# Batch 4's second product as seven products of half blocks

## The chip, the cores and the metric

The kernel runs on one core of a Trainium2 chip. The metric is the device time of one execution in microseconds (us), lower is better; it is compared as the median of several runs. TensorE (PE, with its weight loads PEld), VectorE (DVE), ScalarE (ACT), GpSimd (POOL) and SyncE (SP, which issues all transfers here) run side by side; each takes its own instructions in the order of the program and waits on semaphores for the others.

## What is computed

Attention with a narrow window and block summaries gives x for 4 batches of 768 tokens by 512 channels; then a mix over tokens and two products with weights follow, in float32:

```python
x = attention(q, k, v)                       # (4, 768, 512)
u = x + (x.transpose(0, 2, 1) @ U @ V).transpose(0, 2, 1)
ch = np.maximum(u @ w_ch1, 0.0) @ w_ch2      # 512 -> 2048 -> 512
return (u + ch).astype(np.float32)
```

## The kernel before

**Precision.** Every operand of the two products is split into a high and a low part (a rounded copy by ACT, the rest by a subtraction on DVE or POOL). A product is three matmuls: high by high, high by low, low by high. The channels lie in 4 tiles of 128 (NC), the hidden layer in 16 (NF), a batch's tokens in two halves of 384 (NH).

**Batch 1** (b = 0) does each half of the tokens apart: for f in 0..15 and both halves, `up` (L983, 12 matmuls of 384 columns), `up_out` (ACT's gh at L995, DVE's gl at L996), `down_rows` (L1005, 9 matmuls of 512 columns). Beside it the weights are read as 64-bit words, turned into float32 (L155 on POOL, L161 and L164 on DVE), split (L179 on ACT, L180 on POOL) and stored back to HBM. DVE also makes sums of blocks of the first weight matrix (`sum_weights`, L901 to L905, two additions of 256 columns in each half of an even f). So the later batches load ready sums and only split them.

**Batches 2 to 4** (b = 1 to 3) each have two stages. `up_phase` is the first product by seven products of half blocks (a Strassen-Winograd form): for each of 8 pairs p of hidden tiles, seven products of 6 matmuls of 384 columns (L1271), whose sums ACT and DVE build in a tile (L1293 to L1331). `down_phase` is the second product in the ordinary form: for each f the hidden tile is gated (ACT's gh at L1340, DVE's gl at L1344), and 24 matmuls add to eight banks of PSUM (L1372), 12 of 512 columns and 12 of 256; `leave` (L1395) adds u and sends the output. Weights come through `fetch_weight` (a load into one of three places), `prepare` (the split of half a load, ACT at L179 and POOL at L180, into one of eight places) and `use_weight`; `tick` issues the next load some steps after a load was used up.

**What sets the order.** Everything is emitted by hand, step by step: a generator of the phase yields after each group of matmuls, and between two yields the loop puts the next batch's steps (`later_step`: attention, transposed rows, `mix`; `operands`: the seven operands of the next first product, with L754, L808, L796), spread evenly by `spread`. The last two half-block products of a first product (`last`) run inside the second. In batch 4 no next batch is left, so DVE, ACT and POOL have only the product's own work. Tiles that share a tag share memory; an instruction that writes one waits for the last reader of the tile before it.

## Time and profile before

| what | value |
|---|---|
| median of 3 runs (643.06 to 646.5) | 643.48 us |
| span of the profiled execution, first to last instruction | 644.2 us |
| mean granted TensorE clock, share of full speed | 0.996 |
| PE busy, share of the span | 623.3 us, 97% |
| DVE, ACT, POOL busy | 376.6, 348.2, 362.4 us |
| matmuls | 5480 |

Busy times are unions: a matmul of 384 columns lasts 337 ns from issue to its last result, but the next one starts long before that. So what a matmul costs is read from how many end in a stretch, not from its duration. The same is true of DVE where one instruction follows another without a wait.

### The profile page before, as it was taken

To read this page: it belongs to the slowest core of one execution; us is meant where nothing else is said; L and a number is where in the kernel's file an instruction comes from. 1 tells how busy PE (TensorE), PEld (TensorE's weight loads), DVE (VectorE), ACT (ScalarE), POOL (GpSimd) and SP (SyncE) were. 2 spreads that over 40 slices of the span, in tenths; PEclk is the share of its full clock that TensorE was granted. 3 is DMA by queue.
4 is the path that set the end of the run, shared out by engine and by line. 5 is a ranking of instruction groups with operands and counts; after the bars stand their busy time and mean duration, and the time that the engine had idled before them with its cause. 6 is when DMAs were issued, how large, how long until landed. Compare 5 with 4: busy or idle time off the path is not lost.

```text
span 644.2 us, 14528 instructions
## 1 busy us (share of the span) xinstructions
PE 623.3 (97%) x5480; PEld 560.6 (87%) x5480; DVE 376.6 (58%) x1026; ACT 348.2 (54%) x772; POOL 362.4 (56%) x391
## 2 busy tenths in 40 slices
PE   4979999999999999999999999999999999999997
PEld 3769988889888899998888899998888899998886
DVE  4869777675767596576555845567555722242223
ACT  3756666656564656665543467765453455553220
POOL 3524977965676776772247675772345565653320
PEclk9989999999999999999999999999999999999999
DMA  9897588766676269887786377887743164342102
GB/s 237 212 385 209 166 287 277 226 195 202 196 230 193 67 196 289 245 268 212 235 220 181 105 223 219 263 238 228 237 150 118 59 204 136 115 131 65 34 1 98
DMA packets 74437, 121.67 MB, mean 189 GB/s; under 512 B 7552, under 2 KB 48384, under 8 KB 74368
## 3 DMA queue, kind: packets, MB, share of 16 engines
q1 hardware_dynamic: 74368, 120.75, 61.8%
q8 instruction: 43, 0.70, 0.4%
q14 instruction: 26, 0.21, 0.1%
HBM read 93.45 MB, written 27.26 MB: 187 GB/s over the span
## 4 chain that ended last, share of the span: by engine, by line
PE 87%; DMA 4%; DVE 4%; SPq 2%; ACT 1%; issue 1%; POOL 0%; ACTq 0%; DVEq 0%
PE acc L1372 30%; PE ps_h L1271 27%; PE acc L1005 10%; PE ps_h L983 9%; PE ps_x L517 3%; PE ps_s L374 2%; PE ps_s L351 2%; DMA place<-in_w 2%; PE ps_t L487 1%; DMA kt<-in_k 1%; SPq L215 1%; DMA place<-in_q 1%; DMA place<-in_v 1%; PE ps_m L701 1%; DVE tmp L808 1%
## 5 line engine op out<-in xcount | busy, mean ns | idle before, releaser
L180 POOL TENSOR_TENSOR parts<-whole,parts 128x512 fp32r<-128x512 f32 (+1 forms) x144 | 182.6, 1276 | 153.2 <-ACT parts L179 143.6
L1372 PE MATMUL acc<-gh,parts 128*128 128x256 f32 (+1 forms) x768 | 198.1, 340 | 0.0
L1271 PE MATMUL ps_h<-op,parts 128*128 128x384 f32 x1008 | 181.7, 337 | 0.1
L1271 PEld LDWEIGHTS ps_h<-op,parts 128*128 128x128 f32 x1008 | 174.3, 188 | 2.7 <-issue 1.1
L1372 PEld LDWEIGHTS acc<-gh,parts 128*128 128x128 f32 x768 | 132.8, 189 | 17.9 <-issue 1.7
L1372 PE MATMUL acc<-gl,parts 128*128 128x256 f32 (+1 forms) x384 | 129.9, 338 | 2.5 <-DVE gl L1344 2.5
L1344 DVE SCALAR_TENSOR_TENSOR gl<-place,gh 128x768 fp32r<-128x768 f32 x48 | 52.8, 1101 | 60.7 <-ACT gh L1340 60.4
L179 ACT CAST parts<-whole 128x512 fp32r<-128x512 f32 (+1 forms) x144 | 83.3, 583 | 2.4 <-issue 1.1
L1372 PEld LDWEIGHTS acc<-gl,parts 128*128 128x128 f32 x384 | 72.8, 190 | 9.9 <-DVE gl L1344 3.2
L1340 ACT ACTIVATE gh<-place 128x768 fp32r<-128x768 f32 x48 | 40.5, 845 | 63.8 <-PE acc L1372 60.8
L410 ACT ACTIVATE e<-e,neg 128x120 f32<-128x120 f32 x144 | 46.5, 386 | 52.5 <-DVE neg L400 52.4
L983 PE MATMUL ps_h<-place 128*128 128x384 f32 x384 | 74.2, 341 | 0.0
L983 PEld LDWEIGHTS ps_h<-place 128*128 128x128 f32 x384 | 66.3, 188 | 1.2 <-issue 0.4
L1005 PE MATMUL acc<-place,gh 128*128 128x512 f32 x192 | 67.2, 405 | 0.0
L155 POOL TENSOR_SCALAR val<-place 128x512 f32<-128x512 f32 (+1 forms) x30 | 47.6, 1604 | 25.6 <-ACT place L142 21.4
L180 POOL TENSOR_TENSOR place<-val,place 128x512 fp32r<-128x512 f32 x29 | 38.7, 1353 | 18.3 <-ACT place L179 18.3
L796 POOL TENSOR_TENSOR op<-tmp,op 128x384 fp32r<-128x384 f32 x24 | 25.9, 1088 | 40.3 <-ACT op L792 39.2
L1005 PEld LDWEIGHTS acc<-place,gh 128*128 128x128 f32 x192 | 35.9, 188 | 7.5 <-POOL place L180 0.5
L400 DVE CUSTOM_DVE_ANT_0 e<-ps_s,mask_sb 128x120 f32<-128x120 f32 x144 | 32.7, 276 | 11.4 <-PE ps_s L351 5.9
L1005 PE MATMUL acc<-place,gl 128*128 128x512 f32 x96 | 37.8, 393 | 0.1
L1297 DVE TENSOR_TENSOR place<-place,ps_h 128x384 f32<-128x384 f32 x24 | 13.2, 550 | 36.8 <-PE ps_h L1271 36.8
L1331 DVE TENSOR_TENSOR place<-place,ps_h 128x384 f32<-128x384 f32 x24 | 13.3, 554 | 35.3 <-ACT place L1330 35.2
(122 smaller groups left out, 812.7 us busy)
## 6 DMA issues: line engine op xcount, KB each, us to landing
place<-in_w SPq DMA_DIRECT2D x32, 512.0 KB, 5.3
whole<-up SPq DMA_DIRECT2D x24, 512.0 KB, 4.2
whole<-down SPq DMA_DIRECT2D x24, 512.0 KB, 4.3
whole<-up SPq DMA_DIRECT2D x24, 384.0 KB, 3.5
vt<-in_v SPq DMA_DIRECT2D x48, 146.2 KB, 3.9
kt<-in_k SPq DMA_DIRECT2D x24, 288.0 KB, 5.3
there<-squares SPq DMA_DIRECT2D x16, 384.0 KB, 4.4
at<-there SPq DMA_DIRECT2D x64, 96.0 KB, 3.9
```

Source lines behind the costliest of these rows:

```text
L155: nc.gpsimd.tensor_scalar(f32(bits), f32(hi), 0.0, None, ALU.mult)
L179: nc.scalar.copy(hi, val)
L180: engine.tensor_tensor(lo, val, f32(hi), ALU.subtract)
L400: nc.vector.tensor_tensor_reduce(out=e[:, u, :], in0=ps[:, i * KC : (i + 1) * KC], in1=mask_sb[:, m, :], scale=-SCALE, scalar=BIG, op0=ALU ...
L410: nc.scalar.activation(e[:, u, :], e[:, u, :], AF.Exp, bias=st.neg[h][:, u : u + 1], scale=-1.0,)
L796: engine.tensor_tensor(by_tiles(t[:, 1]), by_tiles(val), by_tiles(f32(t[:, 0])), ALU.subtract)
L983: nc.tensor.matmul(ps[:, :NH], w_split[0, f][:, c % 2, part_w, c // 2], ut[:, c, :], start=(n == 0), stop=(n == 3 * NC - 1),)
L1005: nc.tensor.matmul(acc[t], gt[:, sl], w_split[1, f][:, part_w], start=(first and j == 0), stop=(last and j == 2),)
L1271: nc.tensor.matmul(ps, a[:, sa, i], b[:, sb, i], start=(first and n == 0), stop=(n == 5), skip_group_check=not first,)
L1340: nc.scalar.activation(gh, h, AF.Relu)
L1344: nc.vector.scalar_tensor_tensor(gl, h, 0.0, f32(gh), ALU.max, ALU.subtract)
L1372: nc.tensor.matmul(place, w[:, part_w, c * P : (c + 1) * P], gt[:, q0:q1], start=(f == 0 and i == 0 and j == 0), stop=(f == NF - 1 and j = ...
```

## The change

In batch 4 alone (`SEVEN = (3,)`) the second product is also made by seven products of half blocks. The second weight matrix is cut into blocks of two hidden tiles by 256 output channels. The products, in order, are A11 with B11, A12 with B21, S1 with T1, S2 with T2, S4 with B22, S3 with T3, A22 with T4; A and S are blocks and sums of weights, B and T blocks of the gated hidden layer and their sums. Each has 8 steps of 6 matmuls of 384 columns (4 groups of two hidden tiles, two tiles of 128 output channels).

- **Weights.** In batch 1 DVE makes the sums S1 to S4 (`sum_down`, four additions of 256 columns in each odd f, two in either half) and SP stores them (`store_down_sums`). In batch 3 the split parts of A11, A12 and A22 are stored from their places as they stand (`tick`, 24 transfers), so batch 4 loads them ready. The split of the sums in batch 4 has its low parts on DVE.
- **Operands.** 56 operands (7 names by 8 pairs p) are made by `second_operand`: for T1 to T4 first a sum in place on DVE, then a high part on ACT, then the low part on DVE, which is put behind the next operand's sum. 19 operands are made in the first product (`EARLY`), 6 of the sums for T1 too (`TURNED`). The rest go one or two a step, as far ahead as `lead` and the ring of 33 places allow. ReLU is applied where ACT copies a block out of PSUM, with one more pass for one of the four.
- **Outputs.** After each product DVE adds its two banks to u in x (L1621), or for the last addition of an output into a tile that is sent (L1624): 16 additions in place of the 8 of `leave`, one for each step.
- **Order and places.** Operand and hidden places are cut into two tiles each; transposed rows use operand places in place of hidden ones; for batch 4 the rows, their fetches and the first operands come some steps later in batch 3 (`ROWS`, `FETCH`, `JOIN`).

```diff
+_X = (("A11", "B11", "x"), ("A12", "B21", "y"), ("S1", "T1", "z"), ("S2", "T2", "x"), ("S4", "B22", "z"))
+_Y = (("S3", "T3", "x"), ("A22", "T4", "y"))
+SECOND = {2: (_X[0], _X[2], _X[1], _X[3], _X[4], _Y[1], _Y[0]), 3: _X + _Y}
+ADDED = {
+    "B11": ((0, 0),), "B21": ((0, 0),), "T1": ((1, 1),), "T2": ((0, 1),), "B22": ((0, 1),),
+    "T3": ((1, 1), (1, 0)), "T4": ((1, 0),),
+}
+PARTS = {"A11": (0, 0), "A12": (1, 0), "A22": (1, 1)}
...
+SUMS = ("S1", "S2", "S4", "S3")
+SEVEN = (3,)
...
+PARTS_IN = {1: (), 2: tuple(range(NF // 2))}
+AHEAD_UNITS = (45, 50)
+EARLY = {7 * p + 3 : p for p in range(8)} | {7 * p + 8 : 8 + p for p in range(7)}
+EARLY |= {7 * p + 13 : 16 + p for p in range(4)}
+FIRST_OPERANDS = [EARLY[i] for i in sorted(EARLY)]
+TURNED = {7 * p + 12 : p for p in range(6)}
...
+    ROWS = {2: {16: 0, 18: 1, 25: 2, 29: 3}, 3: {21: 0, 23: 1, 25: 2, 29: 3}}
+    FETCH = {2: {19: 0, 21: 1, 28: 2, 31: 3}, 3: {24: 0, 26: 1, 28: 2, 31: 3}}
+    JOIN = {2: (25, 27, 29, 31), 3: (28, 30, 32, 35)}
...
+        for i, t in enumerate(w_sums[p]):
+            nc.sync.dma_start(out=up_there[p][:, (4 + 4 * i) * P : (8 + 4 * i) * P], in_=t)
...
+        if b in SEVEN:
+            for name, _, _ in SECOND[b]:
+                if name in SUMS:
+                    units += [(("second", name, g), len(loads) + g // 2) for g in range(4)]
+                    loads += [down_sums[:, SUMS.index(name), 4 * j : 4 * j + 4] for j in range(2)]
+                else:
+                    units += [(("second", name, g), None) for g in range(4)]
+            tag_of += [unit_tags[n % 8] for n in range(28)]
...
+        if load is None:
+            _, name, g = key
+            t = wt.tile([P, 2 * DM], F32R, name="parts", tag=tag_of[n])
+            t = t.rearrange("p (m s c) -> p m s c", s=2, c=HC)
+            nc.sync.dma_start(out=f32(t), in_=down_parts[name][:, 2 * g : 2 * g + 2])
+            prepared.append((key, t))
+            return
...
+        split(hi, lo, whole, nc.vector if key[0] == "second" else nc.gpsimd)
         prepared.append((key, t))
+        pass_of = 1 if n < 3 * NF else 2
+        if key[0] == "down" and key[1] // 2 in PARTS_IN[pass_of]:
+            storing.append([3, key[1], t])
         if second:
...
+        for x in storing:
+            x[0] -= 1
+        if storing and storing[0][0] <= 0:
+            _, f, t = storing.pop(0)
+            for name, (odd, half) in PARTS.items():
+                if odd == f % 2:
+                    nc.sync.dma_start(
+                        out=down_parts[name][:, f // 2], in_=f32(t[:, :, half * HC : (half + 1) * HC])
+                    )
         due[:] = [n - 1 for n in due]
...
+    def sum_down(p, n):
+        (a11, a21), (a12, a22) = (
+            (x[:, :HC], x[:, HC:]) for x in (w_kept["down", f] for f in (2 * p, 2 * p + 1))
+        )
+        t = sts[0].x[:, 2 * (p % 3) + n]
+        down_out[p, n] = t
+        x, y = t[:, :HC], t[:, HC:]
+        if n == 0:
+            nc.vector.tensor_tensor(x, a21, a22, ALU.add)
+            nc.vector.tensor_tensor(y, x, a11, ALU.subtract)
+        else:
+            nc.vector.tensor_tensor(x, a12, down_out[p, 0][:, HC:], ALU.subtract)
+            nc.vector.tensor_tensor(y, a11, a21, ALU.subtract)
+    down_out = {}
...
+    def store_down_sums(p):
+        for n in range(2):
+            nc.sync.dma_start(
+                out=down_sums[:, 2 * n : 2 * n + 2, p],
+                in_=down_out[p, n].rearrange("p (m c) -> p m c", c=HC),
+            )
...
+            if st.b in SEVEN:
+                nc.scalar.activation(c[1][:, 0], x, AF.Relu)
+            else:
+                nc.scalar.copy(c[1][:, 0], x)
...
+            nc.scalar.copy(c[0][:, 1], x)
+            if st.b in SEVEN:
+                nc.scalar.activation(c[0][:, 0], c[0][:, 0], AF.Relu)
...
+    def first_sum(st, p):
+        a, b = st.h[p][0][:, 0], st.h[p][0][:, 1]
+        nc.vector.scalar_tensor_tensor(b, b, 0.0, a, ALU.max, ALU.subtract)
...
+    def second_operand(st, m):
+        n, p = divmod(m, NF // 2)
+        block, name, _ = SECOND[st.b][n]
+        c = st.h[p]
+        a, b, c, d = c[0][:, 0], c[0][:, 1], c[1][:, 0], c[1][:, 1]
+        st.gates[m] = hi, lo = st.ring[m]()
+        nv = nc.vector
+        if name == "T1" and p not in st.turned_first:
+            first_sum(st, p)
+        elif name == "T2":
+            nv.scalar_tensor_tensor(b, d, 0.0, b, ALU.max, ALU.subtract)
+        elif name == "T3":
+            nv.tensor_tensor(a, b, a, ALU.subtract)
+        elif name == "T4":
+            nv.tensor_tensor(c, c, b, ALU.subtract)
+        val = {"B11": a, "B21": c, "B22": d, "T1": b, "T2": b, "T3": a, "T4": c}[name]
+        def high():
+            if name == "B22":
+                nc.scalar.activation(hi, val, AF.Relu)
+            else:
+                nc.scalar.copy(hi, val)
+        def low():
+            if name == "B22":
+                nv.scalar_tensor_tensor(lo, val, 0.0, f32(hi), ALU.max, ALU.subtract)
+            else:
+                (nc.gpsimd if m in POOL_LOWS else nv).tensor_tensor(lo, val, f32(hi), ALU.subtract)
+        st.lows.append(low)
+        if len(st.lows) > 1:
+            st.lows.pop(0)()
+        high()
+    def second_start(st):
...
+        for m in FIRST_OPERANDS + [m for m in range(8 * len(OPS)) if m not in FIRST_OPERANDS]:
+            last = 2 * (m // 2) + 1
+            k = min(range(len(places)), key=lambda k: (free_at[k], k))
+            st.ring[m] = places[k][0]
+            st.ready[m] = free_at[k] + 1
+            free_at[k] = last
+        st.order = list(st.ring)
...
+    def second_phase(st):
+        while st.lows:
+            st.lows.pop()()
+        banks = {}
+        for i in range(8 * len(OPS)):
+            g, c = divmod(i, 2)
+            n, q = divmod(g, 4)
+            block, name, to = SECOND[st.b][n]
+            fresh = name not in ("T2", "B22", "T3")
+            if c == 0:
+                w = use_weight("second", block, q)
+            if fresh and q == 0:
+                banks[to, c] = half_bank(f"acc{to}{c}")
+            ps = banks[to, c]
+            for j in range(2):
+                gate = st.gates[2 * g + j]
+                for k, (sa, sb) in enumerate(((0, 0), (0, 1), (1, 0))):
+                    nc.tensor.matmul(
+                        ps,
+                        w[j][:, sa, c * P : (c + 1) * P],
+                        gate[sb],
+                        start=fresh and q == 0 and j == 0 and k == 0,
+                        stop=q == 3 and j == 1 and k == 2,
+                        skip_group_check=not fresh,
+                    )
+            yield
+            for more in range(2):
+                lead = (20 if i % 2 == 0 else -1, 6)[more]
+                while st.order and st.ready[st.order[0]] <= i and st.order[0] <= i + lead:
+                    second_operand(st, st.order.pop(0))
+                    if not more:
+                        break
+            if not st.order:
+                while st.lows:
+                    st.lows.pop()()
+            if late and i > late[0][0]:
+                finish_late()
+            if q == 3:
+                second_out(st, i + 1, n, c, ps)
+            if c == 0:
+                prepare()
+    late = []
+    def finish_late():
+        _, f, *args = late.pop(0)
+        f(*args)
...
+    def second_out(st, i, n, c, ps):
+        def add(mu, nu, ps, last):
+            ch = 2 * mu + c
+            kept = channel_rows(st, ch)[:, 3 * nu : 3 * nu + 3]
+            val = ps.rearrange("p (u q) -> p u q", q=P)
+            if not last:
+                nc.vector.tensor_tensor(kept, kept, val, ALU.add)
+                return
+            o = mo.tile([P, DM], F32, name="o", tag="val", bufs=VALS)[:, :NH]
+            nc.vector.tensor_tensor(o.rearrange("p (u q) -> p u q", q=P), kept, val, ALU.add)
+            late.insert(0, (i, send, ch, nu, o))
+        def send(ch, nu, o):
+            t0 = st.b * S + nu * NH
+            nc.sync.dma_start(out=out[ch, :, t0 : t0 + NH], in_=o)
+        order = [name for _, name, _ in SECOND[st.b]]
+        for to in ADDED[order[n]]:
+            last = not any(to in ADDED[name] for name in order[n + 1 :])
+            late.append((i, add, *to, ps, last))
     def leave(st, acc, q0, q1, channels):
...
+            if b in SEVEN:
+                if i == 0:
+                    second_start(cur)
+                if i in TURNED:
+                    first_sum(cur, TURNED[i])
+                if i in EARLY:
+                    second_operand(cur, cur.order.pop(0))
+                if i in AHEAD_UNITS:
+                    prepare()
+                continue
             if i == UP - 8:
```

In batch 1, around the operands of batch 2 in f = 13, this is what stands on DVE (L161 to L164 make weights, L996 is gl, `tmp` and `op` are operands). Before:

```order
L164 SCALAR_TENSOR_TENSOR val_2215<-place_2068,val_2215 128x512
L996 SCALAR_TENSOR_TENSOR gl_2382<-ps_h_2368,gh_2381 128x384
L808 TENSOR_TENSOR tmp_2409<-x_1456,ps_u_2402 128x384
L808 TENSOR_TENSOR tmp_2410<-tmp_2311,ps_u_2402 128x384
L796 TENSOR_TENSOR op_2235<-ps_u_2402,op_2235 128x384
L161 SCALAR_TENSOR_TENSOR val_2364<-place_2133,val_2364 128x512
L996 SCALAR_TENSOR_TENSOR gl_2442<-ps_h_2428,gh_2441 128x384
L161 SCALAR_TENSOR_TENSOR val_2365<-place_2182,val_2365 128x512
L808 TENSOR_TENSOR tmp_2311<-ps_u_2465,tmp_2410 128x384
```

And in the changed kernel, at the same place:

```order
L180 SCALAR_TENSOR_TENSOR val_2265<-place_2113,val_2265 128x512
L1084 SCALAR_TENSOR_TENSOR gl_2430<-ps_h_2416,gh_2429 128x384
L1050 TENSOR_TENSOR x_120<-val_2148,val_2265 128x256
L1051 TENSOR_TENSOR x_120<-x_120,val_2148 128x256
L824 TENSOR_TENSOR tmp_2460<-x_1482,ps_u_2452 128x384
L824 TENSOR_TENSOR tmp_2461<-tmp_2358,ps_u_2452 128x384
L812 TENSOR_TENSOR place_2457<-ps_u_2452,place_2457 128x384
L177 SCALAR_TENSOR_TENSOR val_2412<-place_2178,val_2412 128x512
L1084 SCALAR_TENSOR_TENSOR gl_2497<-ps_h_2483,gh_2496 128x384
L177 SCALAR_TENSOR_TENSOR val_2413<-place_2230,val_2413 128x512
L1053 TENSOR_TENSOR x_120<-val_2265,x_120 128x256
L1054 TENSOR_TENSOR x_120<-val_2148 128x256
```

Two additions stand behind one gl and two behind the next part of the weights; nothing else moved there.

In batch 4's second product DVE had one gl for each f and, at the end, the output's additions. Before:

```order
L1344 SCALAR_TENSOR_TENSOR gl_7834<-place_7282,gh_7833 128x768
L1344 SCALAR_TENSOR_TENSOR gl_7865<-place_7351,gh_7864 128x768
L1344 SCALAR_TENSOR_TENSOR gl_7896<-place_7351,gh_7895 128x768
L1395 TENSOR_TENSOR o<-acc_7496,x 128x512
L1395 TENSOR_TENSOR o<-acc_7500,x 128x512
```

In the changed kernel, while operands for the fourth product (S2 with T2) are made: L1504 is the sum for T2, L1520 an operand's low part, L196 a weight's low part, L1624 an output's addition.

```order
L1504 SCALAR_TENSOR_TENSOR place_7156<-place_7157,place_7156 128x384
L1520 TENSOR_TENSOR gate_7846<-place_7098,gate_7846 128x384
L196 TENSOR_TENSOR parts_7871<-whole_7665,parts_7871 128x2x256
L1504 SCALAR_TENSOR_TENSOR place_7235<-place_7236,place_7235 128x384
L1520 TENSOR_TENSOR gate_7867<-place_7156,gate_7867 128x384
L1624 TENSOR_TENSOR o_7891<-x_5610,accy0_7796 128x384
L196 TENSOR_TENSOR parts_7893<-whole_7825,parts_7893 128x2x256
L1504 SCALAR_TENSOR_TENSOR place_7316<-place_7317,place_7316 128x384
L1520 TENSOR_TENSOR gate_7887<-place_7235,gate_7887 128x384
```

Each operand's low part now stands behind the sum of the next operand, with a weight's low part and an output's addition between.

On SP in batch 3's second product, transfers for batch 4 (`kt`, `qz`, `there`, `at`, `vt`) and weight loads (`whole`) stood one after another. Before:

```order
L940 DMA whole_5948<-down3_109 128x1024
L435 DMA there_5957<-squares_5918 128x768
L443 DMA at_5959<-there_5769 32x4x192 x4
L229 DMA vt_5987<-in_v 96x390
L230 DMA vt_5987<-in_v 96x390
L940 DMA whole_6006<-down4_110 128x1024
```

In the changed kernel:

```order
L979 DMA whole_6277<-down_113 128x1024
L1027 DMA halfA11_114<-parts_6301 128x2x256
L449 DMA there_6385<-squares_6355 128x768
L457 DMA at_6387<-there_6230 32x4x192 x4
L245 DMA vt_6415<-in_v 96x390
L246 DMA vt_6415<-in_v 96x390
L1027 DMA halfA12_115<-parts_6379 128x2x256
L1027 DMA halfA22_116<-parts_6379 128x2x256
L979 DMA whole_6440<-down_113 128x1024
```

Three stores for each pair of hidden tiles (halfA11, halfA12, halfA22) now stand between them.

## Rows read from the trace of the kernel before

**Rows 1.** Page: busy us (share of the span) xinstructions of the engines.

```profile
PE 623.3 (97%) x5480; PEld 560.6 (87%) x5480; DVE 376.6 (58%) x1026; ACT 348.2 (54%) x772; POOL 362.4 (56%) x391
```

**Rows 2.** Stretches: length, then PE, PEld, DVE, ACT, POOL busy (xinstructions), PEclk, DMA share, GB/s.

```profile
60.00:217.00 157.00, 155.85 (x1236) 138.08 (x1235) 110.94 (x276) 95.39 (x225) 114.85 (x105) 1.00 0.67 209
...
515.28:571.28 56.00, 56.00 (x325) 56.00 (x324) 15.56 (x28) 30.37 (x62) 35.09 (x31) 1.00 0.48 150
571.28:640.42 69.14, 69.14 (x397) 61.05 (x396) 19.65 (x24) 20.19 (x30) 20.45 (x14) 1.00 0.16 54
640.42:644.16 3.74, 0.00 (x0) 0.00 (x0) 0.46 (x2) 0.00 (x0) 0.00 (x0) 0.82 0.43 140
```

**Rows 3.** Waits of PE, whole span: line <- releaser: us in total, times, longest.

```profile
PE acc L1372 <- DVE gl L1344: 2.5, 2, 1.3
```

**Rows 4.** Chain that ended last, in order of time: start us, us, what.

```profile
515.28 56.16 PE ps_h L1271 x324
...
576.31 64.12 PE acc L1372 x372
```

**Rows 5.** DVE in order of time, batch 3's second product: start us, us, instruction.

```profile
479.05 0.56 DVE L754 TENSOR_TENSOR x<-ps_u,place 128x384 f32<-128x384 f32 x1 [0.58 <-PE ps_u L751]
479.65 0.56 DVE L808 TENSOR_TENSOR tmp<-x 128x384 f32<-128x384 f32 x1
480.12 0.55 DVE L808 TENSOR_TENSOR tmp<-tmp,x 128x384 f32<-128x384 f32 x1
480.59 0.55 DVE L796 TENSOR_TENSOR op<-x,op 128x384 fp32r<-128x384 f32 x1
...
505.84 1.56 DVE L808 TENSOR_TENSOR tmp<-x 128x384 f32<-128x384 f32 x1
```

**Rows 6.** DVE by line and form, 511 to 645 us: busy us, mean ns | idle before.

```profile
L1395 DVE TENSOR_TENSOR o<-acc,x 128x512 f32<-128x512 f32 x8 | 5.1, 682 | 1.6 <-PE acc L1372 1.6
L1331 DVE TENSOR_TENSOR place<-place,ps_h 128x384 f32<-128x384 f32 x8 | 4.4, 555 | 17.3 <-ACT place L1330 17.3
```

**Rows 7.** ACT by line and form, 511 to 645 us, same columns.

```profile
L179 ACT CAST parts<-whole 128x512 fp32r<-128x512 f32 x37 | 22.8, 618 | 0.6
...
L792 ACT CAST op<-x 128x384 fp32r<-128x384 f32 x1 | 0.5, 513 | 1.8 <-DVE x L754 1.8
```

**Rows 8.** DVE by line and form, 0 to 217 us, same columns.

```profile
L904 DVE TENSOR_TENSOR place<-val 128x256 f32<-128x256 f32 x8 | 5.4, 678 | 0.0
...
L902 DVE TENSOR_TENSOR place<-place,val 128x256 f32<-128x256 f32 x8 | 4.7, 588 | 0.3
L905 DVE TENSOR_TENSOR place<-val,place 128x256 f32<-128x256 f32 x8 | 4.0, 501 | 0.0
...
L901 DVE TENSOR_TENSOR place<-val 128x256 f32<-128x256 f32 x8 | 4.0, 496 | 0.0
```

**Rows 9.** Waits of all engines, 60 to 217 us, columns as in rows 3.

```profile
DVE gl L996 <- ACT gh L995: 27.3, 20, 3.7
...
PE ps_u L735 <- DVE op L796: 0.4, 1, 0.4
```

**Rows 10.** Chain that ended last, 560 to 645 us: its last piece.

```profile
640.46 0.42 DVE o L1395
```

**Rows 11.** DMA issues, whole span: xcount, KB each, median us to landing.

```profile
whole<-down SPq DMA_DIRECT2D x24, 512.0 KB, 4.3
...
out_t<-o SPq DMA_DIRECT2D x8, 192.0 KB, 1.9
...
out_t<-o SPq DMA_DIRECT2D x4, 128.0 KB, 1.8
```

**Rows 12.** Waits of SP's queue, whole span, columns as in rows 3.

```profile
SPq L940 <- POOL parts L180: 151.8, 41, 10.4
```

**Rows 13.** DMA, 433 to 511 us (batch 3's second product): all queues.

```profile
DMA packets 9094, 12.91 MB, mean 165 GB/s; under 512 B 1028, under 2 KB 6925, under 8 KB 9085
```

221 lines of the change are left out of this document (137 added, 84 removed).

## Prediction, made before the changed kernel ran

> **What bounds the kernel now.** I read the page first: TensorE is busy for 623.3 of 644.2 us [rows 1], so only work taken from TensorE, or idle time given to it, moves the end. Then the stretches [rows 2]. Three matter. In batch 1 (60 to 217 us) TensorE idles 157.00 - 155.85 = 1.15 us, while VectorE works 110.94 of 157: it is the engine with the least room there. In batch 4's first product (515.28 to 571.28) TensorE never idles and VectorE works 15.56 of 56. In batch 4's second product (571.28 to 640.42) TensorE is busy throughout at a granted clock of 1.00 (2.4 GHz), VectorE for 19.65 of 69.14. From the last matmul's end to the end of the span it is 3.74 us. Of TensorE's waits on a matmul of the second products only 2.5 us in all stand in the trace, two of up to 1.3 us [rows 3]. So the removed matmuls lie on the path, and the question is whether what feeds the new ones keeps up.
>
> **The span and the median.** The profiled execution took 644.16 us, 0.68 us over the median of 643.48. I do the sum on 644.16 and take 0.68 off at the end. About 0.5% (3.2 us) is what a measurement of this kernel can tell from no change.
>
> **TensorE's work.** Before: 16 x 24 = 384 matmuls, half of 512 and half of 256 columns, and 12 of the first product's end. A 384-column matmul of the first product ends every 56.16 / 324 = 0.1733 us [rows 4], so those 12 take 2.1 us and the 384 take 69.14 - 2.1 = 67.0 [rows 2]. (The chain's own piece, 64.12 / 372 = 0.172 each [rows 4], would make it 66.2; a few records are missing.) After: 7 x 8 x 6 = 336 matmuls, all of 384 columns with the same forms, 336 x 0.1733 = 58.2 us. Gain 8.0 to 8.8 us, I take **-8.6**.
>
> **VectorE in batch 4's second product.** Here VectorE's work rises from 19.65 us to a stage of its own. Of the 56 operands 19 are made earlier; left are 37 low parts, 26 sums in place (8 for each of T2, T3, T4, 2 for T1), 16 output additions, all of 128x384, and about 15 low parts of weights of 128x512. The price of one: 555 ns is its duration [rows 6], but where nothing is waited for the next one starts earlier: 479.65, 480.12, 480.59, that is 0.47 apart [rows 5]. The sum stands behind the low part of another operand, so most neighbours are independent, and I take 0.475; 128x512 lasts 0.682 [rows 6], by the same overlap 0.60 (an estimate from these rows). Total 79 x 0.475 + 15 x 0.60 = 46.5 us beside 60.3 us of TensorE (58.2 + 2.1). It fits on average, but not everywhere. One product is 8 steps of 6 x 0.1733 = 1.04, 8.3 us. For T2 VectorE needs 8 sums, 8 low parts, 2 output additions and 4 weight parts: 18 x 0.475 + 4 x 0.60 = 10.95, 2.6 over. For B22 without the sums 7.15, 1.2 under. For T3 10.95, 2.6 over. For T4, with four output additions of T3 and no weights, 20 x 0.475 = 9.5, 1.2 over. The lead runs down by 5.2 us in all. How large is it? The code makes one operand every second step while it is more than 6 ahead, so the 19 early ones have melted to a lead of about 6 operands when T2 begins (19 + 24/2 = 31 made at step 24); VectorE idles meanwhile and can't use that time. Six steps are 6.2 us, less one operand's own way of sum 0.555, ACT's high part 0.513 [rows 7], low part 0.555 and the handovers, 1.7: 4.5 us. So TensorE falls short by about 0.7 late in T3 and T4. With 0.46 apart it is nothing, with 0.49 about 2. I take **+1.0**, bounds 0 and 7 (the 7 stands below). ACT has 37 high parts of 0.513 and 15 of 0.618, 28 us in 60, and doesn't bind. POOL has nothing left there; the stretched VectorE instruction of the trace (1.56 us, [rows 5]) lies where POOL works.
>
> The Trainium skill ("VectorE: DVE Perf Modes", section "The DRAIN you can't avoid") says that the next VectorE instruction doesn't start until the pipe has emptied, and the same page gives a float32 tensor_tensor as (N+151)/0.96, which for 384 is an estimate of 557 ns. The duration agrees with 555, the start distances of 0.47 don't; if that rule held for this stream, the first rival below would be the outcome.
>
> **The first product of batch 4.** 25 VectorE operations come in (19 low parts, 6 sums; 12 to 14 us on 15.56 of 56) and on ACT 19 high parts and 8 ReLU passes (some 13.5 us on 30.37). A product waits for ACT's copy of its bank two products (2.1 us) later, and one high part is 0.513, so I cost it at 0. Without that cover: some tenths in each of 8 pairs, up to 2.
>
> **Batch 1.** 32 additions of 128x256 come to VectorE. Their like in L901 to L905 average (678 + 588 + 501 + 496) / 4 = 566 ns [rows 8], so 18.1 us, on 110.94 of 157 [rows 2]: 129, 82%. They are put in odd f only, where the like for the first matrix are absent, so each half now carries what even halves carry already; a half is about 5 us and has two additions, 1.1. Queued behind them are gl, the weights' turn and the operands of batch 2. gl is waited for with 27.3 us of idle VectorE before it in 20 places [rows 9], and TensorE needs it only after the next half's `up` and the other half's `down_rows`, some 4 us later. Once TensorE waited there for VectorE's operand, 0.4 us [rows 9]. I take **+0.6**, bounds 0 and 18.1. SP gets 16 stores of 256 KB and 8 more from the cut of `store_sums`; each waits for additions that lie half an f back, and I cost them at 0 (covered by weight loads issued an f ahead; if not, one landing of some 4 us [rows 11]).
>
> **Batch 3.** SP's queue gets 24 stores of 256 KB (6.3 MB on 12.9 [rows 13], so 246 GB/s in that stretch, above the 209 of batch 1 [rows 2]). Each waits for the split on POOL, for which the loads in that queue wait anyway, 151.8 us in 41 places [rows 12]; behind them stand the transposed squares and rows of batch 4. Rows and first operands also come later, so VectorE has the same operations in fewer steps, though the last gl still has the same neighbours. I take **+0.3**, bounds 0 and 4 (one late landing of 4.3 [rows 11]).
>
> **The tail.** The last addition is 384 columns in place of 256: 0.555 [rows 6] for 0.42 [rows 10]; its transfer is 192 KB for 128 KB, 1.9 for 1.8 us [rows 11]. **+0.2**. Batch 4 loads 20 x 512 KB where it loaded 8, 4.3 us each [rows 11], at DMA shares of 0.48 and 0.16 now [rows 2] and 8 units ahead at most: 0. The finer tiles remove no wait of TensorE that rows 3 show in these stages: 0.
>
> **Sum.** 644.16 - 8.6 + 1.0 + 0.6 + 0.3 + 0.2 = 637.7; less 0.68: **637.0**.
>
> **The rivals.** (1) *VectorE sets the pace of the second product.* If its instructions follow each other at their duration, T2 takes 18 x 0.555 + 4 x 0.682 = 12.7 us, T3 too, B22 8.3, T4 11.1: 11.6 over in all, less 4.5 of lead, 7 us of waits. 637.0 + 6 = 643.0, no change. For it: in-place sums and low parts are chained through ACT, and a waiting instruction starts about 0.55 to 0.6 after the one before (479.05 to 479.65 [rows 5]). Against: neighbours belong to different operands. Chance 0.15. (2) *Batch 1 becomes VectorE's*, the one that ends slower. The additions delay the weights' turn on VectorE, then ACT's and POOL's split, and TensorE waits for weights. In full it costs 18.1: 637.0 - 0.6 + 18.1 = 654.5; the kernel is slower than before from the point at which over 7 us of it reach TensorE, that is when stretched additions use up the 29% that VectorE idles there. Against: even halves show no such waits. Chance 0.08. (3) *SP's queue in batch 3* brings squares or rows late, one landing each time; with two such, 637.0 + 8 = 645, no change. Against: no wait of TensorE for these is in the trace now. Chance 0.07. That the matmuls don't fall is excluded by the order: 336 stand there.
>
> **How the numbers follow.** My forecast holds 0.70, and ends between 634.5 (no waits: 644.16 - 8.8 + 0.2 - 0.68 = 634.9, and a little) and 640.3. The range for 8 in 10 takes in rival 1: 634.5 to 643.5; it leaves out rivals 2 and 3. Faster by over 0.5% (under 640.3): nearly all of the forecast and the milder ends of 1 and 3, 0.70. Within 0.5%: most of 1 and 3 and a tenth of the forecast, 0.20. Slower (over 646.7): 2 and what I don't see, 0.10.
>
> **What would show it.** Right: batch 4's second product lasts about 61 us with 336 matmuls; VectorE is busy there some 45 to 50; TensorE's waits for low parts (L1518, L1520) come to about 1 us and lie in the last third; VectorE's 384-column starts lie 0.47 apart. Batch 1 is within 1 us of its 157. Wrong: many waits of 0.5 us or more from T2 on (rival 1); ACT and POOL idle before weights in batch 1 and TensorE's idle there over 3 us (rival 2); PE waits for `at` or rows in batch 3 (rival 3); or waits for weights loaded ready, which I cost at 0.

## The result, and the profile after

Four runs of the changed kernel have a median of 639.29 us (636.64 to 642.04), four runs of the kernel before beside them 644.99 (643.06 to 647.42); the ratio is 0.9900, 95% interval 0.9854 to 0.9946. (The ratio is not just one median over the other, which is 0.9912 here. Brackets behind a ratio are its 95% interval.) The forecast was 637.0 in a range of 634.5 to 643.5, faster: the time lies in it. That it came so close is in part luck: terms of the sum were wrong by about the same amount on opposite sides.

Windows of the changed kernel by stage (the columns of rows 2): batch 3, batch 4's first product, its second product, the end.

```profile
367.84:514.45 146.61, 145.36 (x1359) 131.20 (x1358) 86.76 (x247) 82.63 (x178) 79.31 (x89) 1.00 0.79 238
514.45:570.46 56.01, 56.01 (x326) 56.01 (x324) 35.77 (x51) 38.60 (x85) 35.34 (x28) 1.00 0.55 173
570.46:631.20 60.74, 60.72 (x349) 60.40 (x348) 48.88 (x97) 27.45 (x55) 0.00 (x0) 1.00 0.44 146
631.20:634.70 3.50, 0.00 (x0) 0.00 (x0) 0.56 (x1) 0.00 (x0) 0.00 (x0) 1.00 0.31 112
```

Against [rows 2]: the second product of batch 4 falls from 69.14 to 60.74 us (-8.40), with TensorE busy throughout; the first product stays at 56.0 although DVE's work in it more than doubles; the end is 0.24 shorter.

Batch 1 is the other place. As its start shifts from one execution to the next (first `up` matmul at 51.98 us in the profile of before, at 49.02 in that of after; with the change the start lay anywhere from 48.4 to 51.9 in other executions), I take it from the first `up` matmul to the end of the last down matmul, and beside it f = 1 alone, from its first `up` matmul to that of f = 2. Windows of before:

```profile
51.98:219.19 167.21, 166.01 (x1286) 147.16 (x1286) 120.02 (x290) 101.57 (x238) 120.97 (x110) 1.00 0.66 206
58.56:68.19 9.63, 9.63 (x56) 8.84 (x54) 8.38 (x19) 4.71 (x13) 8.46 (x10) 1.00 0.47 175
```

and of after:

```profile
49.02:218.41 169.39, 166.57 (x1286) 147.43 (x1286) 136.69 (x323) 101.66 (x238) 124.48 (x110) 1.00 0.74 231
55.89:67.15 11.26, 9.92 (x55) 8.80 (x54) 10.85 (x23) 5.13 (x13) 10.01 (x11) 1.00 0.45 155
```

Batch 1 is 2.18 us longer, 1.63 of it in f = 1, where TensorE never idled before and now idles 11.26 - 9.92 = 1.34. From the end of batch 1 to the end of batch 4's first product it is 352.1 us in both. So with the early start of batch 1 taken out the two profiles differ by -8.40 + 2.18 - 0.24 = -6.46, 1.0%, which is the ratio of the runs.

### The profile page after: what moved, and what is told of

It is laid out like the page before. It is cut to its first block, busy times and chain, and to the rows that moved or that the text cites. A ratio compares the mean times of both kernels' runs of the same rounds, so it can differ in the third digit from the quotient of the medians.

```text
span 634.7 us, 14717 instructions
## 1 busy us (share of the span) xinstructions
PE 614.0 (97%) x5432; PEld 559.1 (88%) x5432; DVE 443.2 (70%) x1154; ACT 364.0 (57%) x820; POOL 346.0 (55%) x375
## 4 chain that ended last, share of the span: by engine, by line
PE 86%; DVE 6%; SPq 2%; ACT 2%; DMA 2%; issue 2%; POOL 0%; ACTq 0%; DVEq 0%; POOLq 0%
PE ps_h L1366 27%; PE acc L1471 20%; PE acc L1093 9%; PE ps_h L1071 8%; PE accx L1584 4%; PE ps_x L529 3%; PE accy L1584 3%; PE accz L1584 3%; PE ps_s L388 2%; PE ps_s L365 2%; PE ps_t L499 2%; SPq L231 1%; DVE tmp L824 1%; DMA place<-in_v 1%; PE ps_m L714 1%
## 5 line engine op out<-in xcount | busy, mean ns | idle before, releaser
L196 POOL TENSOR_TENSOR parts<-whole,parts 128x512 fp32r<-128x512 f32 (+1 forms) x128 | 161.5, 1273 | 116.0 <-ACT parts L195 110.6
L1366 PE MATMUL ps_h<-place,parts 128*128 128x384 f32 x1008 | 181.6, 337 | 0.1
L1366 PEld LDWEIGHTS ps_h<-place,parts 128*128 128x128 f32 x1008 | 174.2, 188 | 2.5 <-issue 1.1
L1471 PE MATMUL acc<-gh,parts 128*128 128x256 f32 (+1 forms) x512 | 135.1, 342 | 0.0
L1471 PEld LDWEIGHTS acc<-gh,parts 128*128 128x128 f32 x512 | 88.9, 189 | 12.7 <-issue 1.7
L1471 PE MATMUL acc<-gl,parts 128*128 128x512 f32 (+1 forms) x256 | 86.7, 339 | 2.6 <-DVE gl L1443 2.6
L195 ACT CAST parts<-whole 128x512 fp32r<-128x512 f32 (+1 forms) x144 | 83.2, 583 | 4.1 <-issue 1.8
L424 ACT ACTIVATE e<-e,neg 128x120 f32<-128x120 f32 x144 | 46.5, 386 | 52.5 <-DVE neg L414 48.0
L1471 PEld LDWEIGHTS acc<-gl,parts 128*128 128x128 f32 x256 | 48.5, 189 | 7.4 <-DVE gl L1443 3.2
L196 POOL TENSOR_TENSOR place<-val,place 128x512 fp32r<-128x512 f32 x29 | 40.6, 1419 | 17.2 <-ACT place L195 17.2
L812 POOL TENSOR_TENSOR place<-tmp,place 128x384 fp32r<-128x384 f32 x24 | 27.2, 1142 | 40.5 <-ACT place L808 35.7
L1443 DVE SCALAR_TENSOR_TENSOR gl<-place,gh 128x768 fp32r<-128x768 f32 x32 | 35.9, 1121 | 17.3 <-ACT gh L1439 16.9
L1084 DVE SCALAR_TENSOR_TENSOR gl<-ps_h,gh 128x384 fp32r<-128x384 f32 x32 | 17.7, 554 | 23.8 <-ACT gh L1083 23.7
L1395 DVE TENSOR_TENSOR place<-place,ps_h 128x384 f32<-128x384 f32 x24 | 13.2, 551 | 30.3 <-PE ps_h L1366 30.2
```

The costliest lines, as they stand in the source:

```text
L195: nc.scalar.copy(hi, val)
L196: engine.tensor_tensor(lo, val, f32(hi), ALU.subtract)
L424: nc.scalar.activation(e[:, u, :], e[:, u, :], AF.Exp, bias=st.neg[h][:, u : u + 1], scale=-1.0,)
L812: engine.tensor_tensor(by_tiles(t[:, 1]), by_tiles(val), by_tiles(f32(t[:, 0])), ALU.subtract)
L1366: nc.tensor.matmul(ps, a[:, sa, i], b[i][:, sb], start=(first and n == 0), stop=(n == 5), skip_group_check=not first,)
L1443: nc.vector.scalar_tensor_tensor(gl, h, 0.0, f32(gh), ALU.max, ALU.subtract)
```

## The experiments

**Batch 1: who pays for the additions.** The changed kernel once more, and two kernels that have either the additions without the seven products or the seven products without the additions. The first, `after_again`:

> The changed kernel once more, against the kernel before in five rounds. In the two profiled executions the second product of batch 4 fell from 69.14 to 60.74 us, 8.4 less, while the medians differ by 5.7. Theory A: nothing else costs anything, and the 5.7 is the spread of single executions (636.6 to 642.0 and 643.1 to 647.4): the ratio comes out at 0.987, 8 us faster, give or take 1. Theory B: the additions and stores of batch 1 give 2 to 3 us back: the ratio stays at 0.991, 6 us faster.

It ran in 637.32 us, ratio 0.9913 [0.9883, 0.9943]. The ratio is the second theory's, while the medians (645.23 for the kernel before) differ by 7.9, the first one's figure: whole runs scatter too much to tell the two apart, and the stretches below have to. The second takes the additions and their stores out; batch 4 reads the first halves of unsummed weights in their place, so its loads stay:

```diff
-                    loads += [down_sums[:, SUMS.index(name), 4 * j : 4 * j + 4] for j in range(2)]
+                    loads += [down_there[:, 4 * j : 4 * j + 4, 0, :HC] for j in range(2)]
...
-                store_down_sums(f // 2 - 1)
...
-                    sum_down(f // 2, 0)
...
-                sum_down(f // 2, 1)
...
-    store_down_sums(NF // 2 - 1)
```

> The changed kernel without the 32 additions and 16 stores of the sums in batch 1; batch 4 loads eight pieces of the stored second weight matrix in their place, so its output is not the reference's, and all else is as in the changed kernel. Theory A: the additions are hidden; the time is that of the changed kernel within 1 us. Theory B: 2 to 3 us faster than the changed kernel, and TensorE's idle time from 60 to 217 us falls from 2.7 us (76.00 - 74.66 and 81.00 - 79.64) to the 1.2 of the kernel before.

The third is the kernel before plus `sum_down` and `store_down_sums`, called at the same points as in the change, and nothing else of it:

> The kernel before with the 32 additions on VectorE and the 16 stores in batch 1 at the places of the change, and nothing else of it; the sums are not used. Theory A: within 1 us of the kernel before, since VectorE idled 29% of batch 1. Theory B: 2 to 3 us slower than the kernel before. In both VectorE's busy time rises by 18 to 19 us.

Without the additions: 636.18 us, 0.9883 [0.9858, 0.9908], by the ratios 1.9 us and by the medians 1.1 under `after_again`. The additions alone: 646.39, 1.0031 [1.0014, 1.0048], by the ratio 2.0 us slower than before, by the medians 1.2. Both lie at or under the lower end of the 2 to 3 us of the second theories, and VectorE's busy time rises by 16.6 us, not 18 to 19. Windows of batch 1 and of f = 1, without the additions:

```profile
50.23:217.80 167.57, 166.29 (x1286) 147.45 (x1286) 119.35 (x291) 101.69 (x238) 121.42 (x110) 1.00 0.66 207
57.09:66.74 9.65, 9.65 (x56) 8.87 (x54) 8.34 (x19) 4.71 (x13) 8.47 (x10) 1.00 0.46 165
```

and with nothing but them:

```profile
49.88:219.02 169.14, 166.31 (x1286) 147.20 (x1286) 136.57 (x323) 101.80 (x238) 124.37 (x110) 1.00 0.73 230
56.73:68.00 11.27, 9.89 (x55) 8.79 (x54) 10.86 (x23) 5.16 (x13) 10.02 (x11) 1.00 0.40 149
```

So nearly 2 us are the price of the additions and their stores: batch 1 of the change is 169.39 - 167.57 = 1.82 longer than without them, 11.26 - 9.65 = 1.61 of it in f = 1. (The other 0.36 that part it from before are there without the additions as well; most lie in f = 0, which takes 6.6 or 6.9 us in executions of the same kernel.) TensorE's longest wait in batch 1 of `after_again` (us in total, times, longest):

```profile
PE ps_s L365 <- ACT kt L347: 1.3, 1, 1.3
```

and DVE, then ACT, in order of time before it (start us, us, instruction), in the same trace:

```profile
59.55 0.55 DVE L1084 SCALAR_TENSOR_TENSOR gl<-ps_h,gh 128x384 fp32r<-128x384 f32 x1
60.02 0.41 DVE L1050 TENSOR_TENSOR x<-val 128x256 f32<-128x256 f32 x1
60.46 1.53 DVE L1051 TENSOR_TENSOR x<-x,val 128x256 f32<-128x256 f32 x1
61.91 0.60 DVE L330 TENSOR_REDUCE km<-kt 128x6 f32<-128x192 f32 x2
...
62.55 0.95 ACT L347 COPY kt<-km 64x48 f32<-64x48 f32 x4 [1.69 <-DVE km L330]
```

The two additions (L1050, L1051) stand in front of the key maxima of batch 2's first head (L330). ACT waits 1.69 us for these, and TensorE 1.33 for ACT's copies. The second addition took 1.53 us for 0.41 of the first. POOL's subtraction (L196) begins at 60.42 in this trace, between the two; `key_first` and `late_f1` below show more of that.

**Batch 1: is it the order?** Three orders. In `key_first` the maxima come one place earlier, ahead of the additions on DVE and, on ACT, ahead of the high parts of the weights:

```diff
-        5: lambda: key_maxima(nxt, 0),
+        4: lambda: key_maxima(nxt, 0),
```

> The changed kernel with the key maxima of batch 2's head 0 put one place earlier, ahead of the f = 1 additions for the down sums on VectorE; nothing else moves. Theory A (batch 1 loses its 2 us at one place: the two additions stand in front of these maxima, ACT's copies of them come late and TensorE waits 1.3 us once on kt): that wait is gone, the stretch from up's matmul of f = 1 to that of f = 2 falls from 11.3 to 9.7-10.0, the whole is 1.3 to 1.6 under the changed kernel (637.3 in the other comparison), ratio to before about 0.989. Theory B (VectorE is simply short of time there): whatever now stands behind the additions comes late instead, the next weights or the next gl, TensorE waits 1 us or more on that, and the time stays within 0.5 of the changed kernel.

638.87 us, 0.9915 [0.989, 0.994]; no gain shows. f = 1 and f = 2 in windows:

```profile
55.16:65.42 10.26, 9.95 (x56) 8.78 (x54) 9.04 (x22) 4.96 (x13) 7.29 (x6) 1.00 0.60 201
65.42:76.67 11.25, 10.64 (x64) 9.43 (x62) 10.08 (x26) 7.02 (x19) 10.82 (x15) 1.00 0.71 223
```

The two waits that are new, 55 to 77 us of that trace:

```profile
POOL place L196 <- ACT place L195: 3.0, 1, 3.0
PE acc L1093 <- POOL place L196: 0.9, 2, 0.6
```

and POOL's subtraction in order of time:

```profile
61.75 2.53 POOL L196 TENSOR_TENSOR place<-val,place 128x512 fp32r<-128x512 f32 x2 [2.97 <-ACT place L195]
```

f = 1 wins 1.0 us (11.23 in `after_again`), f = 2 loses 0.9 (10.37 there): ACT's copies of the maxima now stand ahead of its high parts of the weights (L195), POOL waits 3.0 for these and TensorE 0.9 for POOL. As the expectation's second theory had it, the loss moved, but to what stands behind ACT's copies and not to what stands behind the additions. In this run the two additions took 0.41 and 0.43 us, POOL being idle until 61.75. In the next one all first additions of an odd f stand behind the place, and so behind the maxima on DVE alone:

```diff
-                else:
-                    sum_down(f // 2, 0)
...
             place(4 * f + 2 * hf + 1)
+            if hf == 0 and f % 2:
+                sum_down(f // 2, 0)
```

> The changed kernel with the first two of each four additions for the down sums moved behind the place that follows the down products of the same half, so behind the key maxima of batch 2 in f = 1, while ACT's order is left as it is (high parts of the weights' split, then the copies of the maxima). The run before, which put the maxima first on both engines, won 1.0 us in f = 1 and lost 0.9 in f = 2: ACT's high parts then stood behind the copies, POOL's low parts came late and TensorE waited 0.9 us for these. Theory A (it is a matter of order on the two engines): neither wait is there, f = 1 lasts 9.65 to 9.9 and f = 2 10.4, from the first up matmul to the last down matmul it is 167.6 to 168.0 in place of 169.3, and the whole is 1.3 to 1.7 under the changed kernel beside it. Theory B (the additions take the time wherever they stand): the loss moves again, to gl or the next weights, batch 1 keeps over 169.0 and the two kernels are within 0.5 us.

640.63 us, 0.9924 [0.9899, 0.9949]; the changed kernel beside it, `after_beside`, 639.16, 0.9914 [0.9888, 0.9941]; the intervals overlap.

> The changed kernel once more, beside the run with the moved additions: about 0.991 of before, f = 1 of batch 1 lasts 11.2 to 11.3 us with one wait of 1.3 us on kt, and 169.3 from the first up matmul to the last down matmul, as in the two executions seen so far.

f = 1 is 10.01 in place of 11.26, but f = 2 10.77 for 10.38, f = 5 11.47 for 11.06 and f = 11 11.22 for 10.90; batch 1 is 169.00 against 169.43, and 0.30 of that is f = 0, where nothing was moved. Neither theory had it whole: in f = 1 the order is what counts, elsewhere the change's own places were the better ones, and the sum is about nothing. So the last of the three, `late_f1`, moves the additions in f = 1 alone:

```diff
-                else:
+                elif f > 1:
                     sum_down(f // 2, 0)
...
             place(4 * f + 2 * hf + 1)
+            if hf == 0 and f == 1:
+                sum_down(0, 0)
```

> The changed kernel with the first two additions for the down sums moved behind the key maxima in f = 1 alone; all later additions stand where the change put them. In the run that moved all of them f = 1 won 1.25 us, f = 2 lost 0.4 (the two additions ran beside POOL's subtraction and took 1.45 and 1.38 us each in place of 0.41 and 1.53), and f = 5 and f = 11 lost 0.4 and 0.3. Theory A (each place has its own price, by what stands behind the additions in VectorE's queue): f = 5 and 11 are as in the changed kernel, f = 1 lasts 10.0 and f = 2 10.8, from the first up matmul to the last down matmul 168.5 in place of 169.3. Theory B (the price is VectorE's time in these halves, whatever the order): 169.0 or more. A difference of 0.8 us is under what the medians of whole runs can tell, so the stretch decides.

Windows of batch 1, f = 1 and f = 2:

```profile
48.73:216.99 168.26, 166.50 (x1286) 147.36 (x1286) 136.78 (x322) 101.57 (x238) 123.69 (x110) 1.00 0.75 234
55.32:65.35 10.03, 9.90 (x55) 8.78 (x54) 9.99 (x21) 3.46 (x10) 8.85 (x10) 1.00 0.59 212
65.35:76.10 10.75, 10.53 (x64) 9.40 (x62) 8.94 (x27) 8.03 (x22) 10.36 (x13) 1.00 0.77 230
```

and DVE, then POOL, in order of time, same trace:

```profile
59.59 0.60 DVE L330 TENSOR_REDUCE km<-kt 128x6 f32<-128x192 f32 x2
60.12 1.46 DVE L1050 TENSOR_TENSOR x<-val 128x256 f32<-128x256 f32 x1
61.61 1.39 DVE L1051 TENSOR_TENSOR x<-x,val 128x256 f32<-128x256 f32 x1
...
60.00 2.71 POOL L196 TENSOR_TENSOR place<-val,place 128x512 fp32r<-128x512 f32 x2 [1.06 <-ACT place L195]
```

168.26, 1.1 us better, with f = 5 and 11 as in the changed kernel. Of the 1.1, f = 1 wins 1.2 and f = 2 loses 0.4, which makes the 0.8 that the first theory gave; the other 0.3 lie in f = 0, ahead of what was moved. The additions now run while POOL subtracts (from 60.00 on) and take 1.46 and 1.39 us each. In f = 2 TensorE waits 0.5 us for ACT's `e` (L424), as it does not in `after_again`; that this comes from the stretched additions is not shown. As a whole 637.79 us (636.33 to 639.36), 0.9893 [0.9872, 0.9914]: the best ratio to before among the kernels here that compute everything, but its interval overlaps the changed kernel's, so only the stretch shows the gain.

**Batch 4's second product: how much room VectorE has.** In `eight_early` 8 operands are made in the first product in place of 19, and no sums for T1:

```diff
-EARLY = {7 * p + 3 : p for p in range(8)} | {7 * p + 8 : 8 + p for p in range(7)}
-EARLY |= {7 * p + 13 : 16 + p for p in range(4)}
+EARLY = {7 * p + 3 : p for p in range(8)}
...
-TURNED = {7 * p + 12 : p for p in range(6)}
+TURNED = {}
```

> The changed kernel with 8 of the 56 operands (those of the first product) made early in place of 19, and none of the six sums for T1. So 11 low parts, 6 sums and their high parts move from batch 4's first product, where VectorE is busy 36 of 56 us, into the second, where it is busy 49 of 61. My theory (VectorE is just fast enough, and only the work made ahead keeps it off the path): 17 x 0.469 = 8.0 us more there, and by setting the instructions in their order with starts 0.469 us apart TensorE waits 7.3 us, from the third product on: 60.7 becomes about 68, and the whole is 6 to 8 us slower than the changed kernel. Rival (VectorE has room to spare, the early operands only serve the first steps): within 1 us of the changed kernel.

642.83 us, 0.9978 [0.9959, 0.9997]. Its second product in a window:

```profile
570.24:636.28 66.04, 63.67 (x350) 60.01 (x349) 56.67 (x114) 32.55 (x66) 0.00 (x0) 1.00 0.41 134
```

and the wait of TensorE's weight loads there, by which the gated operands go in:

```profile
PEld accx L1583 <- DVE gate L1519: 5.4, 10, 0.7
```

5.3 us more than the 60.74 of the change: as "my theory" said in kind, if under its 7.3, and the whole is 5.5 us over the median of `after_again`. (Line numbers shift by a few from kernel to kernel: L1583 here is L1584 of the change.) DVE is busy for 56.67 of 66.04, so it isn't full on average; the waits of 5.4 lie on low parts that come too late one by one. Next, one more instruction of 128x384 for every odd operand that isn't made early (`more_dve`), and the same with a larger lead (`more_dve_lead`):

```diff
+            if m not in FIRST_OPERANDS and m % 2 == 1:
+                spare = mask_sb.rearrange("p a k -> p (a k)")[:, :NH]
+                nv.tensor_tensor(spare, val, val, ALU.subtract)
```

> The changed kernel with one more VectorE instruction of 128x384, whose result nothing reads, for every odd one of the operands that are not made early: 18 in batch 4's second product, 18 x 0.469 = 8.4 us more of VectorE. Theory A (VectorE has room on average, 49 of 61 us, but from T2 on it runs without a pause and the lead of 6 operands is all that it has): TensorE waits 3 to 6 us in T3 and T4 (4.4 by working the queue through in order), the stretch is 64 to 66 in place of 60.7, and the whole about 641.7. Theory B (the room is there wherever it is needed): VectorE's 12 idle us take the 8.4, and the time is within 1 of the changed kernel.

```diff
-                lead = (20 if i % 2 == 0 else -1, 6)[more]
+                lead = (20 if i % 2 == 0 else -1, 20)[more]
```

> The same 18 instructions, and the second operand of a step may be made up to 20 ahead in place of 6, so VectorE's early idle time can be used. Theory A (what counts is the order in VectorE's queue: with operands made far ahead the low parts of the down weights stand behind them): more is lost than without the lead, TensorE waits some 8 us, now on low parts of weights as well, the whole is 643 to 647. Theory B (the lead of 6 is what limits): with the lead the idle 12 us take the 8.4, TensorE's waits fall below 1 us and the time is within 1 of the changed kernel.

`more_dve`: 641.27 us, 0.9939 [0.992, 0.9958]. `more_dve_lead`: 651.24, 1.0106 [1.0082, 1.013]. The windows that follow begin at the end of the first product's last matmul; the change:

```profile
575.83:631.00 55.17, 55.17 (x318) 55.02 (x317) 47.86 (x95) 24.95 (x50) 0.00 (x0) 1.00 0.40 127
```

`more_dve`, and under it the waits of its weight loads there:

```profile
577.11:635.40 58.29, 57.94 (x318) 54.55 (x317) 55.59 (x113) 24.95 (x50) 0.00 (x0) 1.00 0.37 117
```

```profile
PEld accy L1587 <- DVE gate L1520: 1.6, 5, 0.5
PEld accx L1587 <- DVE gate L1520: 1.6, 5, 0.5
```

`more_dve_lead`, and the waits of TensorE and its weight loads there:

```profile
576.87:643.10 66.23, 58.75 (x318) 57.67 (x317) 55.89 (x113) 25.00 (x50) 0.00 (x0) 0.95 0.34 106
```

```profile
PEld accz L1587 <- ACT parts L195: 4.4, 1, 4.4
PE accz L1587 <- DVE x L1624: 4.1, 1, 4.1
PE accx L1587 <- DVE x L1624: 3.4, 1, 3.4
```

The spare instructions (19 of them, L1523 in the trace, for the 18 expected) raise DVE's busy time by 7.7 us (47.86 to 55.59) and cost 3.1, within the 3 to 6 of the first theory: the change's own stream had room for some 4.6 us more and no further. With more lead it is worse by another 7.9, 11 us over the change. That is the way the first theory said, but over its 8 us and its 643 to 647, and TensorE waits for other things than it named, high parts of weights and banks in place of low parts of weights. Operands made far ahead stand in DVE's queue before the additions that empty the banks (L1624), and in ACT's before the high parts of the weights (L195). Here the order in the queue is worth more than the room.

**Is POOL, idle there, a help?** The low parts of the late operands go to POOL, 29 of the 37: the 8 of B22 are a scalar_tensor_tensor that the edit leaves on VectorE.

```diff
-POOL_LOWS = ()
+POOL_LOWS = tuple(range(19, 56))
```

> The changed kernel with the low parts of the 37 operands that are not made early on GpSimd (POOL) in place of VectorE: 37 x 0.469 = 17.4 us less for VectorE, some 37 x 1.1 = 41 us on POOL, which has nothing else there. Theory A (two engines side by side): POOL's 1.1 us against a step of 1.04 loses 2 us over 37 operands, which the lead covers; the time is within 1 of the changed kernel and VectorE is busy about 31. Theory B (VectorE's instructions stretch while POOL works, as one addition in batch 1 did, 0.41 to 1.53 us): VectorE stays as busy as before or busier, both come late, TensorE waits over 3 us in T2 to T4, and the whole is over 640.5.

642.96 us, 0.9969 [0.9949, 0.9989]: the second theory. The stretch from the first product's last matmul on, 5.1 us longer than in the change, and the longest wait of TensorE's weight loads in it (5.4 us of such waits in all, nearly all for POOL's low parts):

```profile
577.45:637.70 60.25, 57.49 (x318) 54.70 (x317) 47.90 (x67) 24.86 (x50) 31.25 (x28) 1.00 0.37 117
```

```profile
PEld accx L1584 <- POOL gate L1520: 3.6, 5, 1.1
```

DVE by line there, and POOL's low parts one by one and then without a pause:

```profile
L196 DVE TENSOR_TENSOR parts<-whole,parts 128x512 fp32r<-128x512 f32 x16 | 14.9, 934 | 9.1 <-ACT parts L195 9.1
L1508 DVE TENSOR_TENSOR place<-place 128x384 f32<-128x384 f32 x8 | 9.6, 1252 | 0.0
L1506 DVE TENSOR_TENSOR place<-place 128x384 f32<-128x384 f32 x8 | 6.8, 899 | 0.0
```

```profile
603.38 1.01 POOL L1520 TENSOR_TENSOR gate<-place,gate 128x384 fp32r<-128x384 f32 x1 [1.64 <-ACT gate L1514]
622.40 7.78 POOL L1520 TENSOR_TENSOR gate<-place,gate 128x384 fp32r<-128x384 f32 x6
```

DVE has 28 instructions less (67 for 95 in the stretch) and is busy for 47.90 us as before: its sums for T4 (L1508) and its weight parts stretch to 1.25 and 0.93 us as a mean, from 0.55 and 0.69. POOL's own instruction stretches too, from 1.01 us to 1.30 (7.78 / 6) beside these sums, and 1.30 is over the 1.04 of a step: so the low parts come late.

**Batch 3: do the stores cost?** In the first profiles batch 3 took as long as before, 146.5 us:

```profile
368.65:515.12 146.47, 145.23 (x1359) 130.93 (x1357) 87.44 (x247) 82.45 (x178) 79.34 (x89) 1.00 0.65 195
```

In later ones of kernels that are the same there it took up to 148.6, once 150.4, with waits of TensorE for the transposed squares `at` (`after_beside`, window of batch 3: 148.60, one wait of 1.1). In `twice_stored` each of the 24 stores is issued a second time, to memory that nothing reads:

```diff
+                    nc.sync.dma_start(
+                        out=spare_parts[name][:, f // 2], in_=f32(t[:, :, half * HC : (half + 1) * HC])
+                    )
```

> The changed kernel with each of the 24 stores of weight parts in batch 3 issued twice, the second time to memory that nothing reads: 6.3 MB more in SP's queue, 256 KB each. In the executions so far batch 3 (first matmul of its first product to that of batch 4's) took 146.5 us in both with the old weights and 146.1 to 148.6 with the stores, once 150.4; where it took 147.8 or more, TensorE waited 1 to 2 us for vt and for the transposed squares at, which come through the same queue. Theory A (these waits come from the stores, which keep the squares and values back in the queue): with the stores doubled the waits grow, batch 3 lasts 150 to 155, and the whole is 3 us or more over the changed kernel. Theory B (they are a spread of the transfers, whatever the stores): batch 3 stays within 146 to 149 and the whole within 1 us of the changed kernel.

647.54 us, 1.0048 [1.0025, 1.0071]; some 8 us over the change by the ratios, 7.0 of it in batch 3. Its window:

```profile
370.26:523.77 153.51, 146.92 (x1358) 132.40 (x1357) 86.77 (x247) 82.67 (x178) 79.22 (x89) 0.99 0.87 268
```

and TensorE's wait for the squares in it, 0 in the change's first profile:

```profile
PE ps_x L529 <- DMA at<-there: 5.3, 3, 2.2
```

So 48 stores do keep the squares back. For the 24 of the change it is not shown: eleven profiled executions with them range from 146.5 to 150.4 and average 147.5 us, against 146.5 in both without, about 1 us. The change also puts rows and their fetches later in batch 3 (`ROWS`, `FETCH`), and no run has that without the stores. What tells a quick execution from a slow one is open.

## Why the prediction was right, point by point

- **TensorE's work, -8.6.** Right: -8.40 in the second product, within 8.0 to 8.8. The chain has six runs of 48 matmuls of 8.32 to 8.40 us, two of them here (chain of after, order of time), so 0.174 each for the 0.1733 of [rows 4]. (The lower bound of 8.0 stood on a wrong reading: the 372 of [rows 4] are all 384 but 12, not a piece with a few records missing, and the 12 are of 512 columns, so 0.172 each is too little for the whole.)

```profile
597.78 8.32 PE accx L1584 x48
606.10 8.36 PE accz L1584 x48
```

- **VectorE in the second product, +1.0.** Too high: no wait of TensorE stands in that stretch. The busy time (48.88 for 45 to 50) and the pace were right. The wait that I drew from them did not come: I put the lead of the operands a little short, by 0.7 us, and it was enough. DVE in order of time in T3 (after):

```profile
605.90 0.55 DVE L1518 SCALAR_TENSOR_TENSOR x<-place,x 128x384 fp32r<-128x384 f32 x1
606.37 0.55 DVE L1621 TENSOR_TENSOR x<-x,accx 128x384 f32<-128x384 f32 x1
606.84 0.69 DVE L196 TENSOR_TENSOR parts<-whole,parts 128x512 fp32r<-128x512 f32 x1
607.44 0.55 DVE L1518 SCALAR_TENSOR_TENSOR gate<-place,gate 128x384 fp32r<-128x384 f32 x1
```

  Starts are 0.47 apart (0.60 behind a 128x512) at durations of 0.55 and 0.69. I took 0.475, and wrote that 0.46 would give no wait at all and 0.49 about 2: the term lay inside its own bounds. Rival 1 (a pace of 0.555) is refuted by these starts. The rule that the prediction takes from the Trainium skill ("VectorE: DVE Perf Modes", "The DRAIN you can't avoid") is only half of what that section says: it goes on that a next instruction which is not held starts earlier. The trace agrees with that half, 0.47 from start to start at a duration of 0.55. How much was left `more_dve` shows: some 4.6 us of the 12 that VectorE idles.
- **Batch 4's first product, 0.** Right as a time (56.01), wrong in its working: DVE's added work is 20.2 us, not 12 to 14, since the early low parts run beside POOL (L1520 there averages 1129 ns, in the second product 552); ACT's is 8.2, not 13.5. The cover held for more of VectorE than I had asked of it.
- **Batch 1, +0.6.** This step failed: 2.18 in the profiles, 1.82 against the kernel without the additions, inside the bounds of 0 to 18.1 but not within the 1 us that I gave as a sign of being right. I named gl, the weights' turn and the operands as what is queued behind the additions, and argued by the 4 us that gl has. I left out the key maxima of batch 2, which stand behind them once, in f = 1, and whose reader TensorE needs at once. I also took a mean of 566 ns where the stretched one that mattered lasts 1.53. In even halves no such waits stand; but the key maxima aren't in an even half. I also called VectorE the engine with the least room there, at 110.94 of 157; in [rows 2] POOL has less, at 114.85, and it is beside POOL's work that the additions stretch. Of rival 2 the mechanism (the weights' turn late on VectorE) didn't happen as the change stands; in `key_first` TensorE did wait 0.9 us for weights, but because ACT's copies stood ahead of them.
- **Batch 3, +0.3.** 0 in the profile of the change, about 1.0 over eleven: within 0 to 4. Rival 3's mechanism is shown for twice the stores only.
- **The tail, +0.2.** -0.24: the span ends 3.50 us after the last matmul, for 3.74.
- **The span and the median, -0.68.** Mis-sized. A run's time is its span plus about 1.9 us (634.7 and 636.64 in the first run of the change), so the profiled execution of before, 644.16, belongs to a run of some 646.1, 2.6 over the median of 643.48; batch 1 began at 51.98 us in it, and at 48.4 to 51.9 in the thirteen other profiles. Before's median in the six comparisons was 644.28 to 645.58, so the forecast of 637.0 was built on a time that is some 1.5 us low; that is most of the 2.3 between it and 639.29.

The sum of the terms without the offset was -6.5, and -6.46 is what the profiles differ by; that agreement is luck, since VectorE's term, the tail and batch 3 were 1.7 too dear, and batch 1 was 1.6 and TensorE's work 0.2 too cheap.

## What to carry to other kernels

When instructions are put into an in-order queue, list every instruction behind them in each place until the next idle time, not only those of the stage that they belong to: one reader that the bound engine needs at once is dearer than thirty that have slack. A stage without waits can be tested for its room by adding spare instructions to it: VectorE at 49 of 61 us busy took some 4.6 us more here, not 12. Work given to an idle engine may slow its neighbour by as much as it takes over, as in `pool_lows`.
